# Linear attention and a routed attention layer on one core: casts in SBUF moved to ScalarE and GpSimd, constants moved, fewer warming products, other first loads, a new order

## The chip, the core and the metric

The kernel runs on one core of a Trainium2 chip. The metric is the device time of one execution in microseconds (us); the median of three runs of the kernel before is 534.78 us (534.38 to 536.3). Engines are called PE (TensorE; PEld is its weight load), VectorE (DVE in the rows), ScalarE (ACT), GpSimd (POOL) and SyncE (SP, whose queue issues most DMAs).

## The reference

Two layers follow each other. `qt`, `kt` below are q and k, laid out by the host with the head dimension first; all data is float32.

```python
def phi(x):                                    # 8 batches, 8 heads, 576 rows, head dim 64
    proj = einsum('bhsd,df->bhsf', x, w_phi)   # 128 features
    proj = proj - max(abs(proj), axis=-1, keepdims=True)
    return concatenate([exp(proj), exp(-proj)], axis=-1)
q_p, k_p = phi(q), phi(k)
kv  = einsum('bhsf,bhsd->bhfd', k_p, v);  z = sum(k_p, axis=2)
x   = (q_p @ kv) / (q_p @ z + 1e-6)            # heads side by side: 8 x 576 x 512
logits = x @ w_gate                            # 4 experts, the best 2 of a row, softmax over the 2
for e in range(4):
    q, k, v = x @ wq[e], x @ wk[e], x @ wv[e]
    a  = causal softmax(q @ k.T / 8)
    ye = a @ v @ wo[e]
    out += weight of e for this row (0 if not chosen) * ye
```

## The kernel before

The first layer is done for 32 pairs of heads p (4 pairs to a batch). For k: products with w_phi (`stream_k` for 1024 rows, `stream_tail` for the last 128), on VectorE the maxima of |proj| (L410) and their subtraction (L412), on ScalarE two exponentials (L189), then the products with v (`stream_kv`, L424 and L488). For q: a product with w_phi (`stream_q`; for p below 5 straight from float32, from p = 5 on with q split in a high and a low part, cast at L502 and subtraction at L183), copies from PSUM (`evac_u`), a maximum over partitions on GpSimd (L532), its subtraction (L542), two exponentials, and the products with kv (`stream_n`). `divide` normalises (L455, L464), `turn_x` transposes on VectorE (L577), writes to HBM and reads back as x, casts x to its high part (L589) and subtracts for the low part (L591, in L183). The second layer is done for 8 batches b: projections of q, k, v and the gate from x in high and low parts (L178), scores (L675), softmax (`soft`, `post`, with maxima on GpSimd at L532, subtractions at L806), products with v, `norm_y`, `move_y` (transpose, HBM, cast to the high part at L863, subtraction at L865), `project_out` and `store`. Weights are loaded in pieces and split likewise (`split_piece`).

What a cast in SBUF may run on is asked of `copies_sb` (L205); before it is the same as `copies`, ScalarE or VectorE. The cast of q (L500) asks `copies`, and so do copies from PSUM.

The order of the work is written out. Each piece of work is a generator ("stream") that yields its steps. `Plan.loop` reads the string PICKS two letters at a time: the first letter says which of the streams that are alive goes on (by its place in the list), the second which PSUM banks a step gets or, where a step leaves the engine open, whether it takes the first (a value below 8) or the second. At the start the streams stand in this order: A load_phi, B keep_warm, C load_k, D load_q, E load_v, F stream_k, G stream_tail, H stream_q, I to K the weights, then kv, n, s; a stream that ends leaves the list. `in_order` then holds each engine, and the queue SP, to this order. A reduction on GpSimd also waits for the last VectorE operation marked `port` ahead of it (L530).

Before the loop VectorE sets up constants: memsets (L212 to L273), and 14 operations that make `ident` and `mask` (L215 to L227; the tile is written into ek1). `keep_warm` issues groups of three products of a constant tile (L341); with WARM_AT the first four pairs' k products stand behind such groups.

How often each open choice falls on an engine by the two lists:

| operation | before | after |
|---|---|---|
| cast of x | ScalarE 27, VectorE 5 | ScalarE 12, GpSimd 20 |
| cast of y | ScalarE 12, VectorE 2 | ScalarE 5, GpSimd 9 |
| cast of q (pairs 5 to 31) | ScalarE 20, VectorE 7 | ScalarE 20, VectorE 7 |
| pieces of qk and wo | ScalarE 5, VectorE 1 | ScalarE 4, GpSimd 2 |
| pieces of vg | ScalarE 2 | ScalarE 2 |
| 64-column scaling of x | ScalarE 45, VectorE 19 | ScalarE 41, VectorE 23 |

The first real products on PE by the lists. Before: ten warming groups, q0, k0, the tail of k0, eight warming groups, q1, q2, k1, tail 1, kv0, tail 2, k2, num0, kv1. After: eight warming groups, k0, tail 0, q0, q1, q2, k1, tail 1, kv0, tail 2, k2, num0, kv1. Ahead of the first projection (after kv7 and the tail of k8) both lists hold the same products.

## Time and profile before

| | |
|---|---|
| median of three runs | 534.78 us (534.38 to 536.3) |
| the profiled execution: span from its first to its last instruction | 532.6 us; the page gives no time beside the span |
| busy | PE 522.5, PEld 505.7, DVE 496.5, ACT 389.6, POOL 195.5 us |
| granted TensorE clock | 1.000 |

In the rows below, times are us from the span's start unless marked ns. A line of a timeline merges like instructions (x is their count) and may end with the idle time of the engine before it and what released it. A group line gives busy time and the mean ns of one. PE's ends are modelled, so a busy PE is not PE at its peak.

### The profile page before, as it was taken

How to read it: one execution, taken by the hardware profiler on the slowest of the kernel's cores; microseconds unless marked ns; L12 is line 12 of the kernel's file. 1: busy time of each engine (PE TensorE's matmuls, PEld its weight loads, DVE VectorE, ACT ScalarE, POOL GpSimd, SP SyncE). 2: the span in 40 equal slices, each digit the busy share in tenths (PEclk: the TensorE clock that was granted, in tenths of full speed). 3: DMA queues.
4: the chain of work that ended last, by engine and by line, in shares of the span. 5: the costliest groups of instructions: out<-in, count | busy, mean ns of one | idle time of the engine just before them, and what ended most of it. 6: DMA issues, size and time to landing. Idle time of an engine off the chain costs nothing. (4 is left out here: it accounts for less than half of the span.)

```text
span 532.6 us, 22043 instructions
## 1 busy us (share of the span) xinstructions
PE 522.5 (98%) x9452; PEld 505.7 (95%) x9452; DVE 496.5 (93%) x1061; ACT 389.6 (73%) x723; POOL 195.5 (37%) x76
## 2 busy tenths in 40 slices
...
GB/s 203 200 202 181 199 151 118 97 146 123 147 162 100 147 77 164 188 148 191 105 114 163 106 119 169 116 199 132 117 99 159 121 82 127 112 122 101 69 90 90
DMA packets 102674, 72.68 MB, mean 136 GB/s; under 512 B 57137, under 2 KB 84145, under 8 KB 102577
## 3 DMA queue, kind: packets, MB, share of 16 engines
...
q8 instruction: 74, 1.21, 1.0%
q10 hardware_dynamic: 384, 0.39, 0.3%
...
## 5 line engine op out<-in xcount | busy, mean ns | idle before, releaser
L532 POOL PARTITION_ALL_REDUCE mx<-u x32 | 126.9, 3985 | 139.6 <-ACT u L187 54.1
L178 PE MATMUL ps_c<-xb,qk 128*128 128x320 f32 (+1 forms) x768 | 109.0, 296 | 0.0
L178 PEld LDWEIGHTS ps_c<-xb,qk 128*128 128x128 f32 x768 | 103.0, 188 | 1.5 <-issue 0.2
L189 ACT ACTIVATE ek<-ek 128x1152 f32<-128x1152 f32 x64 | 74.8, 1170 | 5.6 <-DVE ek L412 3.8
L424 PE MATMUL ps_c<-v_in,ek 128*64 128x65 f32 x2048 | 72.0, 222 | 1.7 <-ACT ek L189 1.4
L424 PEld LDWEIGHTS ps_c<-v_in,ek 128*64 128x64 f32 x2048 | 67.5, 137 | 3.5 <-ACT ek L189 1.8
L532 POOL PARTITION_ALL_REDUCE tops<-top x15 | 54.2, 3612 | 45.0 <-DVE top L714 22.0
L189 ACT ACTIVATE st<-st 128x1152 f32<-128x1152 f32 (+3 forms) x60 | 50.8, 872 | 15.4 <-DVE st L806 15.4
L806 DVE TENSOR_TENSOR st<-st,tops 128x1152 f32<-128x1152 f32 (+4 forms) x75 | 58.3, 812 | 3.0 <-POOL tops L532 2.9
L187 ACT COPY st<-ps_c 128x512 f32<-128x512 f32 (+1 forms) x101 | 45.9, 510 | 15.7 <-DVE ps_c L701 9.8
L187 ACT COPY u<-ps_c 128x320 f32<-128x320 f32 (+3 forms) x120 | 44.3, 416 | 13.7 <-PE ps_c L515 9.2
L178 PE MATMUL ps_c<-yh,wo 128*128 128x256 f32 (+1 forms) x256 | 53.0, 299 | 0.3 <-ACT yh L187 0.3
L178 PE MATMUL ps_c<-vg,xb 128*128 128x260 f32 x384 | 50.2, 284 | 0.0
L424 PE MATMUL ps_c<-vl,st 128*64 128x65 f32 x1500 | 48.8, 222 | 0.0
L412 DVE TENSOR_TENSOR ek<-ps_c,pmax 128x128 f32<-128x128 f32 (+1 forms) x64 | 47.5, 745 | 1.4 <-PE ps_c L424 0.6
L410 DVE TENSOR_REDUCE pmax<-ps_c 128x8 f32<-128x1024 f32 (+1 forms) x64 | 47.5, 747 | 0.9 <-PE ps_c L370 0.2
L178 PEld LDWEIGHTS ps_c<-vg,xb 128*128 128x128 f32 x384 | 47.9, 188 | 0.4
L424 PEld LDWEIGHTS ps_c<-vl,st 128*64 128x64 f32 x1500 | 47.1, 138 | 0.5 <-issue 0.2
L542 DVE TENSOR_TENSOR u<-u,mx 128x1152 f32<-128x1152 f32 x32 | 43.5, 1360 | 0.1
L178 PEld LDWEIGHTS ps_c<-yh,wo 128*128 128x128 f32 x256 | 40.8, 188 | 1.2 <-ACT yh L187 0.4
L189 ACT ACTIVATE u<-u 128x1152 f32<-128x1152 f32 (+3 forms) x36 | 40.7, 1139 | 0.6 <-DVE u L806 0.4
L424 PE MATMUL ps_c<-kv,u 128*64 128x65 f32 x1152 | 39.8, 222 | 0.8 <-issue 0.8
...
## 6 DMA issues: line engine op xcount, KB each, us to landing
...
q_in<-in_qt_dram SPq DMA_DIRECT2D x58, 144.0 KB, 3.3
...
k_in<-in_kt_dram SPq DMA_DIRECT2D x31, 160.0 KB, 3.6
...
```

The costliest lines, as they stand in the source:

```text
L178: nc.tensor.matmul(o, a, b, start=start, stop=stop, skip_group_check=True)
L187: nc.scalar.copy(o, i)
L189: nc.scalar.activation(o, i, func, **kw)
L410: nc.vector.tensor_reduce(out=m, in_=src, axis=AX.X, op=ALU.max, apply_absolute_value=True)
L412: nc.vector.tensor_tensor(out=to, in0=src, in1=m.unsqueeze(len(m.shape)).to_broadcast([*m.shape, 128]), op=ALU.subtract)
L424: nc.tensor.matmul(o, a, b, start=start, stop=stop, skip_group_check=True)
L532: nc.gpsimd.partition_all_reduce(o, i, 128, op)
L542: dve(2 * S, [uk], [mk], port=True).tensor_tensor(out=U, in0=U, in1=M, op=ALU.subtract)
L806: dve(2 * n, [sj[j]], [*key, mk], port=True).tensor_tensor(out=a, in0=a, in1=tops[x][0:m, :, 128 * j:], op=ALU.subtract)
```

## The change

- `copies_sb`, the choice for casts of x, y and weight pieces in SBUF, becomes ScalarE or GpSimd (`copies_sb`, `copy`); the loop takes the engine from the step's own pair.
- Memsets of tri, cnt, v_in, xq, yq and vl move from VectorE to GpSimd. The 14 operations for `ident` and `mask` stay on VectorE, but are issued by the first step of `stream_b(0)`, into a tile of the scores.
- WARMS is 8 instead of 18, and no k product waits for a warming group.
- k of pair 0: upper half and tail part on SP, lower half on ScalarE's queue (all three on ScalarE's before). q of pair 0: its second head on ScalarE's queue.
- PICKS is another list.

```diff
@@ -31,8 +31,8 @@
 XT_RATE = 1.085
 IB = 2
 Q0 = 5
-WARMS = 18
-WARM_AT = (7, 11, 14, 17)
+WARMS = 8
+WARM_AT = ()
 
 
 NPAIRS = B * NP
@@ -51,49 +51,49 @@
 
 CODE = "ABCDEFGHIJKLMNOPQRSTUVWXYZabcdefghijklmnopqrstuvwxyz0123456789-_!#$%&()*+,./:;<=>?@[]^`{|}~' §¶µ¿¡ßæøåçðþ"
 PICKS = (
-    "BADAAABABABABABABAIAIIBABAIACABAHIAAJAOAHaQIPAF-GAAANIIACACAIAHAABOAHAABABABABABABABOAOANAAAFIOICAFaNADAMAFsFIGANAQADANI"
-    "D-AACAMAMAPAGAOABAQAQAOAMAMANAECJDJAEAAAJIGAOAPAOADADADsPAOAOADADAK-CAKAJAJAEBOAOAOAOAOIFaFsBAMAJAGAPAAABASASICAD-QAQAMA"
-    "FsHATAFaAAMAGASAOANAPAPAQADAOAMAMADADIFIFAJFJAPABAK-KAJACAECNAPAOAOAJDJAQACATAQASAQAMAPAJAPIFsFIPASAFARADAAAPADADaRAK1KA"
...
+    "BEBHBEBABFBFBBBGAABACACACAHAEsBAFDOAAAAANACAFIF-NANAFaFININANAF-RAPAGAAAMAOIMAFaNIDARAHACADAGAPIMADIEFPABAAABANAOAJEJAEH"
+    "MAQAPAQAOAPAGAJAMADAHADADaOAPAOAOADADAKsKAOAOAOIMAJGJAECCAFIFjJAD-GATARAOAHAAAQASIGARAOABAQAFjFIMASAUACAAAGARAPAOAQAOAJF"
+    "JANAQAMAPAFADADAFADaEBK-KAQAJARAQAJAJAFsFaBAPAMAMAQACAAAMACAHAPAPAPAJANAPAGAUAPANADASADAOADIEDK-KAUAFIQIFAQAQANAJCJAQASA"
...
 )
 
 
@@ -138,7 +138,7 @@
             s, x = self.streams[CODE.index(i)], CODE.index(x)
             assert s[1].pred is None or s[1].pred()
             if isinstance(s[1].eng, tuple):
-                s[1].eng = 'DVE' if x >= 8 else 'ACT'
+                s[1].eng = s[1].eng[x >= 8]
             if not self.advance(s, self.take(s[1], x) if s[1].tag else None):
                 self.streams.remove(s)
         assert not self.streams
@@ -196,50 +196,52 @@
     def copy(eng, n, o, i, w, r, rate=1.04):
         if eng == 'ACT':
             act(n, o, i, w, r)
+        elif eng == 'POOL':
+            nc.gpsimd.tensor_copy(o, i)
         else:
             dve(n, w, r, rate, rate < 1).tensor_copy(o, i)
 
     def copies(n):
         return 'ACT', 'DVE'
 
-    copies_sb = copies
+    def copies_sb(n):
+        return 'ACT', 'POOL'
 
     def load(o, i, w, r=(), rate=90.0):
         nc.sync.dma_start(o, i)
 
     ek2 = [sb(f"ek{i}", [128, 2, NU, 128]) for i in range(EKB)]
-    col, row, warm = ek2[1][:, 0, 0], ek2[1][:, 0, 1, 0:32], ek2[1][:, 1, 8, 0:64].bitcast(BF16)
+    warm = ek2[1][:, 1, 8, 0:64].bitcast(BF16)
     nc.vector.memset(warm, 1.0)
     for i in range(BANKS):
         nc.vector.memset(plan.both[:, i, NJ * V1 - 1:512], 0.0)
-    nc.vector.memset(col[:, 0:1], 0.0)
-    for k in range(7):
-        n = 2 ** k
-        nc.vector.tensor_scalar(out=col[:, n:2 * n], in0=col[:, 0:n], scalar1=float(n), scalar2=None, op0=ALU.add)
-    nc.vector.transpose(row, col[:, 0:32])
-    for k in range(1, 4):
-        r_ = slice(32 * k, 32 * k + 32)
-        nc.vector.tensor_scalar(out=row[r_, 0:1], in0=row[r_, 0:1], scalar1=32.0 * k, scalar2=None, op0=ALU.add)
-    ident = sb("ident", [128, 128])
-    nc.vector.tensor_scalar(out=ident, in0=col, scalar1=row[:, 0:1], scalar2=None, op0=ALU.is_equal)
-
-    mask = sb("mask", [128, 128])
-    nc.vector.tensor_scalar(out=mask, in0=col, scalar1=row[:, 0:1], scalar2=-1.0e9, op0=ALU.is_lt, op1=ALU.mult)
-    tri = sb("tri", [128, 4, 4])
-    nc.vector.memset(tri, 0.0)
+    ident, mask = sb("ident", [128, 128]), sb("mask", [128, 128])
+    tri, cnt = sb("tri", [128, 4, 4]), sb("cnt", [128, 5, 4])
+    nc.gpsimd.memset(tri, 0.0)
     for a in range(3):
-        nc.vector.memset(tri[:, a, a + 1:4], 1.0)
-    cnt = sb("cnt", [128, 5, 4])
+        nc.gpsimd.memset(tri[:, a, a + 1:4], 1.0)
     for e in range(4):
-        nc.vector.memset(cnt[:, :, e:e + 1], float(3 - e))
+        nc.gpsimd.memset(cnt[:, :, e:e + 1], float(3 - e))
+
+    def constants(col, row):
+        nc.vector.memset(col[:, 0:1], 0.0)
+        for k in range(7):
+            n = 2 ** k
+            nc.vector.tensor_scalar(out=col[:, n:2 * n], in0=col[:, 0:n], scalar1=float(n), scalar2=None, op0=ALU.add)
+        nc.vector.transpose(row, col[:, 0:32])
+        for k in range(1, 4):
+            r_ = slice(32 * k, 32 * k + 32)
+            nc.vector.tensor_scalar(out=row[r_, 0:1], in0=row[r_, 0:1], scalar1=32.0 * k, scalar2=None, op0=ALU.add)
+        nc.vector.tensor_scalar(out=ident, in0=col, scalar1=row[:, 0:1], scalar2=None, op0=ALU.is_equal)
+        nc.vector.tensor_scalar(out=mask, in0=col, scalar1=row[:, 0:1], scalar2=-1.0e9, op0=ALU.is_lt, op1=ALU.mult)
 
     k_in = [sb(f"k_in{i}", [128, KC]) for i in range(IB)]
     q_in = sb("q_in", [128, S])
     v_ins = [sb(f"v_in{i}", [128, 10, V1]) for i in range(2)]
     for t in v_ins:
-        nc.vector.memset(t[:, :, 64:V1], 1.0)
+        nc.gpsimd.memset(t[:, :, 64:V1], 1.0)
         for h in range(2):
-            nc.vector.memset(t[64 - 64 * h:128 - 64 * h, 8 + h, 64:V1], 0.0)
+            nc.gpsimd.memset(t[64 - 64 * h:128 - 64 * h, 8 + h, 64:V1], 0.0)
     wf = sb("wf", [128, WP])
     wfs, qs = sb("wfs", [128, 2, WP], F32R), [sb(f"qs{n}", [128, S], F32R) for n in "hl"]
     kv = [sb(f"kv{i}", [128, 4, V1]) for i in range(2)]
@@ -253,7 +255,7 @@
     xd = [dp.tile([128, S], F32, name=f"xd{i}") for i in range(2)]
     xt = [sb(f"xt{i}", [128, 4, 32 * NJ]) for i in range(2)]
     for t in xq:
-        nc.vector.memset(t[64:128, :, 128:160], 0.0)
+        nc.gpsimd.memset(t[64:128, :, 128:160], 0.0)
     xB = [sb(f"xb{i}", [128, 2, S], F32R) for i in range(PXB)]
     xT = [[t[:, n] for n in range(2)] for t in xB]
     xE = sb("xe", [128, NP, 128], F32R)
@@ -265,12 +267,12 @@
     yt = [sb(f"yt{i}", [128, 4, 32 * NJ]) for i in range(2)]
     yd = [dp.tile([128, S], F32, name=f"yd{i}") for i in range(2)]
     for t in yq:
-        nc.vector.memset(t[64:128, :, 128:160], 0.0)
+        nc.gpsimd.memset(t[64:128, :, 128:160], 0.0)
     q2 = [sb(f"q{p}", [128, S], F32R) for p in "hl"]
     kk2 = [sb(f"kk{p}", [128, S], F32R) for p in "hl"]
     vl = sb("vl", [128, NJ, 4, 66])
-    nc.vector.memset(vl[:, :, :, 65:66], 1.0)
-    nc.vector.memset(vl[64:128, NJ - 1], 0.0)
+    nc.gpsimd.memset(vl[:, :, :, 65:66], 1.0)
+    nc.gpsimd.memset(vl[64:128, NJ - 1], 0.0)
     lg = vl[:, :, :, 0]
     vlo_ge = sb("vlo", [128, 4, 65])
     vlo, ge = vlo_ge[0:64], vlo_ge.rearrange("p a b -> p (a b)")[:, 0:80].rearrange("p (t a b) -> p t a b", t=5, a=4)
@@ -349,11 +351,11 @@
 
     def load_k():
         for p in range(NPAIRS):
-            yield Step('SP' if p else 'ACT', pred=(lambda: ('main_k', p - IB) in done and ('tail_k', p - IB) in done) if p >= IB else None)
-            x, q = k_in[p % IB], nc.sync if p else nc.scalar
-            q.dma_start(x[0:64, :], kt[p][:, 0:KC])
-            q.dma_start(x[64:128, 0:512], kt[p][:, 768:1280])
-            q.dma_start(x[64:128, 512:KC], kt[p][:, 640:768])
+            yield Step('SP', pred=(lambda: ('main_k', p - IB) in done and ('tail_k', p - IB) in done) if p >= IB else None)
+            x = k_in[p % IB]
+            nc.sync.dma_start(x[0:64, :], kt[p][:, 0:KC])
+            (nc.sync if p else nc.scalar).dma_start(x[64:128, 0:512], kt[p][:, 768:1280])
+            nc.sync.dma_start(x[64:128, 512:KC], kt[p][:, 640:768])
             done.add(('load_k', p))
 
     def raw_q(p):
@@ -363,7 +365,7 @@
         for p in range(NPAIRS):
             yield Step('SP', pred=(lambda: ('proj_q', p - 3) in done) if 3 <= p < Q0 else has('proj_q', Q0 - 2) if p == Q0 else has('split_q', p - 1) if p > Q0 else None)
             for h in range(2):
-                load(raw_q(p)[64 * h:64 * h + 64, :], qt[p][:, S * h:S * h + S], ('q_in', h), rate=60.0)
+                (nc.sync if p or not h else nc.scalar).dma_start(raw_q(p)[64 * h:64 * h + 64, :], qt[p][:, S * h:S * h + S])
             done.add(('load_q', p))
 
     def half_mm(o, a, b, n, w, r):
@@ -741,6 +743,8 @@
 
         left = [13]
         yield Step('PE', (), None, all_x(b * NP))
+        if b == 0:
+            constants(st[0][1][:, 0, 0:128], st[0][1][:, 0, 128:160])
         for g in range(2):
             for sel in range(2):
                 for s0, s1 in PARTS:
```

## Rows read from the trace of the kernel before

**Rows 1.** The page, part 1: busy us, share of the span, instructions.
```profile
PE 522.5 (98%) x9452; PEld 505.7 (95%) x9452; DVE 496.5 (93%) x1061; ACT 389.6 (73%) x723; POOL 195.5 (37%) x76
```
**Rows 2.** Busy time by stage: PE, PEld, DVE, ACT, POOL, granted clock, DMA share, GB/s.
```profile
15.08:66.02 50.94, 49.02 (x1273) 45.99 (x1271) 48.50 (x87) 46.68 (x74) 27.77 (x7) 1.00 0.78 195
66.02:529.36 463.34, 461.88 (x8068) 449.76 (x8066) 434.75 (x917) 336.31 (x638) 163.65 (x64) 1.00 0.49 128
```
**Rows 3.** Waits of PE: who for whom, us in total, times, longest.
```profile
PE ps_c L424 <- ACT ek L189: 1.4, 1, 1.4
```
**Rows 4.** Timeline of 54 to 67 us: start, us, engine, line (VectorE, GpSimd, PE).
```profile
56.50 0.45 DVE L200 CAST xb<-xb 128x576 fp32r<-128x576 f32 x1
...
57.20 2.67 DVE L200 CAST xb<-xb 128x576 fp32r<-128x576 f32 x1
59.79 1.21 DVE L410 TENSOR_REDUCE pmax<-ps_c 128x8 f32<-128x1024 f32 x1
...
57.12 4.15 POOL L532 PARTITION_ALL_REDUCE mx<-u  x1 [4.38 <-ACT u L187]
...
63.51 1.15 PE L424 MATMUL ps_c<-v_in,ek 128*64 128x65 f32 x32 [1.40 <-ACT ek L189]
```
**Rows 5.** Timeline of the first 16 us.
```profile
1.13 0.53 ACTq L354 DMA_DIRECT2D k_in<-in_kt_dram  x1
1.29 3.36 PE L178 MATMUL ps_c<-ek 128*128 128x128 bf16 x30 [1.29 <-DVE ps_c L214]
...
2.75 1.42 DVE L218 TENSOR_SCALAR ek<-ek 128x1 f32<-128x1 f32 x7
...
5.03 0.28 DVE L227 TENSOR_SCALAR mask<-ek 128x128 f32<-128x128 f32 x1
...
6.49 0.27 PE L370 MATMUL ps_c<-wf,k_in 64*128 64x128 f32 x1
...
7.23 0.46 DVE L200 CAST qk<-ot 128x576 fp32r<-128x576 f32 x1
...
9.47 1.50 PE L178 MATMUL ps_c<-ek 128*128 128x128 bf16 x24 [1.05 <-DVE u L200]
...
10.08 1.42 DVE L410 TENSOR_REDUCE pmax<-ps_c 128x8 f32<-128x1024 f32 x2
...
13.92 1.07 PE L370 MATMUL ps_c<-wf,k_in 64*128 64x128 f32 x16
...
15.08 1.07 PEld L424 LDWEIGHTS ps_c<-v_in,ek 128*64 128x64 f32 x32
```
**Rows 6.** DMA issues: count, KB each, median us from issue to landing.
```profile
q_in<-in_qt_dram SPq DMA_DIRECT2D x58, 144.0 KB, 3.3
...
k_in<-in_kt_dram ACTq DMA_DIRECT2D x1, 160.0 KB, 4.4
```
**Rows 7.** Groups by form: busy us, mean ns, idle before.
```profile
L577 DVE STREAM_TRANSPOSE xt<-xq 128x640 f32<-128x640 f32 x32 | 26.5, 832 | 0.6 <-ACT xq L189 0.6
L455 DVE TENSOR_TENSOR xq<-ps_c,rd 128x256 f32<-128x256 f32 x64 | 25.8, 416 | 0.5
...
L187 ACT CAST xb<-xb 128x576 fp32r<-128x576 f32 x27 | 18.0, 673 | 0.6 <-DMA xb<-xd 0.4
...
L464 DVE TENSOR_SCALAR xq<-ps_c,rd 64x64 f32<-64x64 f32 x19 | 5.2, 276 | 0.2
```
**Rows 8.** GpSimd's copies (ns min/median/max), and one beside a VectorE subtraction.
```profile
L689 POOL COPY top<-st x15: 396/462/764, 84.6 to 494.0; 128x256 f32<-128x256 f32 x15
...
L792 POOL COPY gw<-gw x8: 179/317/1177, 100.5 to 517.3; 64x2 f32<-64x2 f32 x8
...
160.65 1.35 DVE L542 TENSOR_TENSOR u<-u,mx 128x1152 f32<-128x1152 f32 x1
...
160.86 1.18 POOL L792 COPY gw<-gw 64x2 f32<-64x2 f32 x1 [0.79 <-DVE gw L789]
```
**Rows 9.** Timeline of the end, PE.
```profile
521.71 0.50 PE L178 MATMUL ps_c<-yh,wo 128*128 128x256 f32 x2 [0.30 <-ACT yh L187]
```

More of the change, by code (lines that the diff above doesn't have):

```diff
@@ new lines @@
+    "rArAqApAFIrAY-mApApAnAsADAqAqApApADArALAKAKACAmAmADalAPAOBLAlAlAQEPFnAoAKAoAjAlAlAmAfAgAfAjAeAFAmAKAiAFAMBOHfAkAlAcALAMG"
+    "LCiAdAdAdAcAdAdAdAIsEDIAdAjAjAdAjAfAiAHGHADAHAHDfAAAfAgAeIgAZABAaAAAgAgALAgAfAEHIsIAZAhAKAiAiAiAhAaIGILADAbAcAdAaAeAeAeA"
+    "JAHAEG7ALALAbAbAbAbAHA6A5A5ALs7A5ALa9A9AD-5A5A5I6A6AFaFI9A8AbAbALsLa7A7A6A6AFADAaIDADI7AaAeGdH4AAACACA9A5A9A6A9A5A5A5A9A"
+    "FA6AdBcABAKA3A3A6A2A2A5ADA4AFsFa9AYA5ADAFA3AzA0AyAZA2AD-6A4IzA2A0A2AHBHAHAzAzAIaHEEFzAHAIA3AzA2AzAHAIIIAI-5AAAFA3AzA3A3A"
@@ new lines @@
+    "3I3A3I2AzAzAzAzAzaEE4AZAYAXABAwAIA0AyAWAWACADAyA2A1A1A1ADA1AzAzAzA1A1IzAwAwAwAwA0A0AFsF-2A2I2A2A0A0A0AhIhsh-wA3A6A5A5Ahs"
+    "zADazA3AFAGAFA7A1A3A1A3A6A1A0AdAaB3A0AzA0AWAzAzAzAcAXCsAbD0IYHpAzA0ADAuAvAzAyAoAAAoIoAxAYAxIpAqACAAAYGsAvAvAuAuAnAGAGAqA"
+    "YAWAJArAXFlADADR,AqA+ABAmAFjF-.AoAnAHAHACAnA.A.A.AmAHA.AlImIXAoAFApApApApApAHDHAI-IAHApApA*AXApApA)AXAosEAoA)AIaoAmAoA(A"
+    "FA+AEBoAIA(A*AkA(A.ADA(ADAHAHAmA(A*A+A*A,A,A,A*A*A*I*A(AXRX-+A)I,ADsGA)IGA*A*AFIFa+I+A.A,A+AkA.AW-WIpDAACABA*AFA+A+A+A,A"
@@ new lines @@
+    "FABA(A)AmC&A)A(A)A,A(A)A,A)AmFDA+A&A_A)AFjFI,A+A,A&AlA_A(A(AKHkGLEFA7A#IFAFaFI-A&A$A%A%ADA&A_A_A_A_A$A_A_A_A_A_ADsHaHAEB"
+    "GH*A$A)A9AAABAGAGA-AFA$A!A&A%A7A9ACAhA9A7A9I9A9A9A9A!A$AFA$A!A$A8AgABACAAAHsEH#A#ADA_A_I_A%A6A_AHA$A$ADA$A9A#A#I#A#AmAFa"
+    "$A-AD-qsFR!A8AnA%A7A%A&AlBJCKA9A3A9A8I8Am-DA!A8A8A_AFIFAFa-A9A8A6A7A-A9A9ADAmsmI9A8IF-8A8I8I!A2A!A9A!A1IDaGGGAEH9A9A8A8A"
+    "JAdABAxAQAwA5A9A5AwA8A3A8AKFIAeEMAKBLDcCGIJA`AuA1AAAyADA[A@IaDtACApArA>AvAwA>A>AwA?AvAYHvAvAvAvAvA=AFIyAZAvAXG<ADAXDDIHs"
@@ new lines @@
+    "HAFA=AXAoA=A=A=A:A<A<A<A/AqAqIXA:AnA:AsApAoAoAAAGCGAGAssGGGAqA/AGAmIKABAsAWApAlAmAmI*A)AkAoACAmAHaEG(A(ADAEAHAmAmAmA(A)A"
+    "mAH-HA*A(A(A&A+A&A&AlA(AkA%ADAGCGAFI&A&I)AGAJAAA#A(A(I%A%A&A&IF-VsDa)A*A(A(AFI)A#ACAFA)A)AVIF-+A+A*A,A+AVsFIV-)A+ABADA)A"
+    ")A)A*A)I#A)A+AFA+ADA)ADanBkAAAMEkF%I%A%AKGJH%A&A&A%A&A&A%AgAeA5ACAeA7A8AeB7A8AECGD6AFA#A!A!AGAEEH-HA6A8A8A8A8A8A8A8A%A!A"
+    "8A-A2AGA_A#A_A2A9I8A8A8A8A8A!A9A8A4A9A8ADADA8A8A8IFa_I_Aoso-oa#A#A_A_A_A9A9A9A9A9I_AD-7AFs!AoI!A!AKE%AjFeE0AzAJAAAJA8A5A"
@@ new lines @@
+    "6A7A5A5A7A0AKGfH0A2A2A3A3AMDJCtIwADA8A6AYAxAwAwAyAyAzAZHKB4A2IYCBAvAuA0IwAwAwAyAwAZDYG1AFAxAuAuA0I1AXCtAoAH1HA1AtAtAsAuA"
+    "vAxAJACAmApAWAWAIAFAWAoAmAGAGApIWAmAtAJAlABArAqAnAqAojGApIkApAEH*AoAlIoIoAmADAnAlACAmAmAHIHAkImAmA&A%A%A%AmA%I%A(A(AGCGA"
+    "%AGAjA&A&A&A&AVIV-FaVskA*A*AF-+A(A(I(I)A)A)A*IFAVI)A(A&A(A&ADaFA)A)AKG,A(A%A%A*A&A&AnHmGmEMFJAjBAA!A7A#A!A-A9A!AiACA7AAA"
+    "7A-ADADA#A&A9A$ADa!A!A#AGHEGGAHs-AGA-A-A-A#A-A9A!A!AHAHa!A--HA!A9A9A9A_A_ADADA-A-I-AEBBAiAhA8A8A8AAA8A!A-A-A-A-I-A7A#A!A"
```

60 lines of the change are left out of this document (20 added, 40 removed).

## The prediction

> **What bounds the kernel now.** I read the page's table of busy shares first, then the busy time by stage, then who waited for whom, then the timelines of the stretch before the first projection and of the first 16 us. The table shows PE at 98% of the span and its weight loads at 95%, VectorE at 93%, ScalarE at 73%, GpSimd at 37% [rows 1]. PE is the bound over all, and a change that leaves its products as they are wins only where PE has holes. By stage [rows 2], PE is busy for 461.88 of 463.34 us from the first projection (66.02) to its last product (529.36): no hole worth a name, though VectorE is close behind with 434.75. The holes lie before 66 us. From 15.08 to 66.02 PE, VectorE and ScalarE are all above 91%, so that a stall of any of the three reaches PE.
>
> **What holds the stage before 66 us.** The largest single wait of PE with real work is 1.4 us for an exponential of k [rows 3]; it is the idle time in front of the products of kv at 63.51 [rows 4]. Followed back on VectorE: its cast of x at 57.20 took 2.67 us where the one at 56.50 took 0.45; GpSimd's reduction had started at 57.12; the maxima of k for pair 7, at 59.79, were queued behind that cast, then their subtraction, the exponential and PE behind these [rows 4]. So one cast in SBUF by VectorE cost VectorE 2.67 - 0.45 = 2.2 us and PE 1.4. At the start, VectorE's real work begins at 7.23 with the cast of a weight piece and reaches the first maxima of k only at 10.08; the first weight load of kv is at 15.08 [rows 5].
>
> The Trainium skill, "SBUF — State Buffer", section "Who interferes with whom", says that VectorE's copies and casts in a two-port mode, and its operations with two SBUF inputs, exclude a GpSimd operation that reads SBUF, and that the second to start waits until the first is done. The trace agrees that there is such a wait, not that it lasts to the end: the cast was done at 59.87, the reduction at 61.27.
>
> **The change, part by part.** Which operation runs where, and in what order, I read from the two lists of picks against the streams.
>
> 1. *First loads.* The list puts pair 0's k first: its main and tail products, then q0, q1, q2. Before, wf and the three parts of k were issued one behind the other on ScalarE's queue, k from 1.13 on, and the k products started at 6.49 [rows 5]. Now the upper half of k is first on SP, with the tail part behind it, and the lower half stands second on ScalarE's queue, where the first part of k was issued at 1.13. Landing took 4.4 us for such a part and 3.3 for one of q [rows 6], so k is there at 4.4 to 5.6. Its 20 products take about 1.4 us (the 16 of pair 1 took 1.07, [rows 5]) or twice that at half the clock: VectorE's first work comes at 6.0 to 8.0, against 7.23; taken -0.3. What is pushed back on SP are the weight pieces; v and pair 1's k come sooner than before, since fewer weight pieces stand ahead of them.
>
> 2. *VectorE's work before the first projection.* Both lists do the same products on PE before it, so VectorE's lists can be set side by side. Out go five casts: a weight piece 0.46, q5 and q8 2 x 0.46, x0 0.45 and x1 2.67, together 4.50 [rows 4, 5]. In come a cast of q6, 0.46, and the 14 operations for ident and mask, which ran from 2.66 to 5.31, thus 2.65 [rows 5]. That is -1.39. Copies from PSUM balance (one of u in, one of kv out). Four scalings of 64 columns fewer at 0.28: -1.1 [rows 7]. Put off until after the projection: a division's two multiplications at 0.42 and four smaller operations, about 1.8; drawn ahead: one transpose, 0.83; net -0.9 [rows 7]. Sum: **-3.4**. The memsets given to GpSimd are worth nothing of themselves, since VectorE had no data until about 7 us. The constants are the bad half: they leave a time in which VectorE had nothing else and enter one where it is full; the list has them behind the subtraction for pair 7's k, so that neither they nor a cast of x stand ahead of the exponential that PE waited for.
>
> 3. *Casts on GpSimd.* By the list 20 of 32 of x, 9 of 14 of y and 2 of weight pieces; ScalarE loses 15 of x and 7 of y, 22 x 0.67 = 15 us [rows 7]. A cast of 128x576 on GpSimd is not in the trace. From the nearest rows, 64x2 in 0.18 us and 128x256 in 0.40, it comes to 0.67 on a line through both, and in proportion to the second's median of 0.46 to 1.04 [rows 8]. I take 0.75, near the line, whose ends are the undisturbed runs. That GpSimd waits for VectorE is seen: the copy of 64x2 took 1.18 us beside a two-input subtraction of 1.35 [rows 8]. That such a subtraction waits for a copy is not in the trace: 0 to 1.04 us for each. Four of the casts lie before the first projection (x0, a weight piece, x1, x2): 0 to 4.2, taken **+0.7**, as subtractions are about a third of VectorE's operations there. The other 27 lie in the body, where x is cast for the next batch, and VectorE is idle for 463.34 - 434.75 = 28.6 us: taken 0. Behind a cast on GpSimd mostly a reduction is queued; GpSimd is idle for 63%.
>
> By the skill's rule every cast that a subtraction meets would hold it for the rest of the cast; with all four met in full, 4 x 0.75 = 3.0 instead of 0.7, the forecast would be 534.2.
>
> 4. *Warming products.* 24 instead of 54. The granted clock of the rows is 1.00 throughout [rows 2], but the first 30 took 3.36 us, 112 ns each, which is 128 columns at about 1.2 GHz, and the 24 at 9.47 took 1.50 us, 62 ns, the level of 2.4 GHz [rows 5]. Now they end at about 1.29 + 24 x 0.112 = 4.0, 0.4 to 1.6 us before k. The rise may come later, which costs 0 to 1.4 us, held in item 1's range. The second bundle filled a hole, and leaving it out gains nothing.
>
> 5. *PE's side.* The chain to the first products of kv, from k's products done at 6.9 in VectorE's new order: small maxima, a small subtraction, small centring, a copy, and at 8.4 the maxima (1.2), a copy (0.48) and the centring (1.2), done at 11.4; the exponential (1.17) at 12.6; kv at 12.9 against 15.08: -2.2. With the 1.4 us of [rows 3] gone too PE could be 3.6 ahead at the projection; VectorE's sum allows 0.3 + 3.4 - 0.7 = 3.0. The smaller holds, less some idle time of VectorE between 7 and 9 us, where it follows PE closely: **-2.7**.
>
> 6. *The end.* Two output products of the batch before now stand in front of the transposes of the last y; PE waits 0.3 us for a cast there [rows 9]: **-0.2**. What follows PE's last product, a copy and the store, stays.
>
> Sum: -2.9 on a span of 532.64, so 529.7. The page gives no time beyond the span; the median of the runs, 534.78, stands 2.14 above it, and with the same 2.14 the forecast is **531.9 us**.
>
> **Rivals.**
> - *The gain is eaten.* Waits for GpSimd's casts and the constants take back VectorE's saving (item 3 at +2.5): for it, VectorE is at 95% there [rows 2]; against it, the list puts the constants where x is still on its way. -1.1: 533.7. Chance 0.21.
> - *The body gets denser too.* ScalarE has 15 us less to do, and no cast of x on VectorE meets a reduction. Against it: PE shows only 1.5 us of idle time there. Another -3: 528.9. Chance 0.13.
> - *The clock stays low.* If PE pauses too much until about 12 us, its some 5 us of products ahead of kv run at half rate, most of it hidden behind VectorE: +2, 533.9. Chance 0.07.
> - *Slower: the last x of a batch.* Its cast stands on GpSimd behind a reduction of 3.9 us [rows 4], or blocked by VectorE, and VectorE's subtraction and the next projections wait for it. At 0.9 us of PE in each of 7 batches: +6.3 - 2.9, 538.2. From 0.4 us a batch on the sign turns. For it: PE and VectorE are both full. Against it: six buffers of x give half a batch of lead. Chance 0.13.
> - *Not what the words say.* The diff leaves the line of q's cast (L500) between ScalarE and VectorE, and the list gives VectorE 7 of 27, as before: no time of its own, but a meeting like that at 57.20 stays possible for q.
>
> **Numbers.** The forecast has 0.46. About 0.5%, 2.7 us, is what a measurement of this kernel can tell from no change. Of the forecast's own spread (529.5 to 533.5) two thirds lie below 532.1, which with the denser body gives faster 0.44; the slower rival and the tails of the others give slower 0.17; the rest is 0.39. Range 528.0 to 537.0: low with items 2 and 5 in full and a part of the denser body, high with five batches of the slower rival.
>
> **What would show it.** k's first product at about 5 us and kv at about 13; no VectorE cast of x, and no hole of PE ahead of pair 7's kv; the first projection at 63 to 64; GpSimd's casts at 0.7 to 0.8 us with VectorE's subtractions of x still at 0.75; from there to PE's last product 463 us, as before. It is wrong if that last stretch differs by more than 2 us either way, or the first projection stays at 66.

## The result and the profile after

The changed kernel took **540.62 us** (median of 4 runs, 540.09 to 541.59); the kernel before took 534.58 us beside it. The ratio is 1.0108, with an interval from 1.0081 to 1.0135: 6 us slower, where 531.9 was forecast. The time lies outside the range given.

The page of the kernel after, its span and its table of busy time, answers to [rows 1]: VectorE has 3 us more than before, and ScalarE 16 us less.

```profile
span 539.7 us, 22005 instructions
PE 526.3 (98%) x9422; PEld 506.7 (94%) x9422; DVE 499.7 (93%) x1038; ACT 373.9 (69%) x695; POOL 220.5 (41%) x127
```

The first projection came as early as forecast. From the timeline of the kernel after: k's first products at 5.04, the first small maxima of k at 7.69, the products of kv at 13.67 (their first weight load at 13.56, against 15.08), the first projection at 63.15 against 66.02 [rows 2, 4, 5]. No cast of x runs on VectorE. The constants (L230) stand on VectorE just ahead of the projections.

```profile
5.04 2.08 PE L372 MATMUL ps_c<-wf,k_in 64*128 64x128 f32 x16
7.69 0.29 DVE L412 TENSOR_REDUCE pmax<-ps_c 128x1 f32<-128x128 f32 x1 [5.03 <-PE ps_c L426]
...
13.67 1.10 PE L426 MATMUL ps_c<-v_in,ek 128*64 128x65 f32 x32
...
58.26 2.49 DVE L230 TENSOR_SCALAR st<-st 128x1 f32<-128x1 f32 x7
58.74 1.34 POOL L200 CAST xb<-xb 128x576 fp32r<-128x576 f32 x2
...
63.15 3.02 PE L178 MATMUL ps_c<-xb,qk 128*128 128x320 f32 x15
```

The body is where the time went. Before, it took 463.34 us from the first projection to PE's last product [rows 2]; after, that last product ends at 536.35, so it took 536.35 - 63.15 = 473.2 us. The busy times by stretch show where. Two rows of the kernel after, 143 to 190 us and 190 to 529, and behind them the first of these stretches of the kernel before; columns are PE, PEld, DVE, ACT, POOL with their instructions, the granted clock, the DMA share and GB/s:

```profile
143.00:190.00 47.00, 43.21 (x785) 41.37 (x786) 44.78 (x84) 32.52 (x62) 18.12 (x8) 0.96 0.38 103
190.00:529.36 339.36, 337.41 (x5858) 327.72 (x5854) 318.82 (x680) 222.92 (x422) 131.58 (x67) 1.00 0.47 126
```
```profile
143.00:190.00 47.00, 46.44 (x931) 45.15 (x931) 45.02 (x90) 39.98 (x75) 18.29 (x7) 1.00 0.51 129
```

In these 47 us PE did 785 products instead of 931 (not all of the same kinds; the table further down weighs them), with 3.8 us of holes and part of the stretch at a lower clock. The timeline of the kernel after there, from top to bottom: a reduction of GpSimd starts at 145.27, and y's subtraction, 0.41 us behind it, takes 2.30 us. A second reduction starts at 155.44, and the third subtraction of the scores, on 64x128, takes 2.52 us; the same line is done in 0.27 elsewhere. The centring of k (161.73) is queued on VectorE behind it, PE waits for that 2.16 us, and then its products run at half rate (56 in 3.08 us, against 1.84 in the first run below); the granted clock of the 7 us from 164 is 0.76.

```profile
145.27 3.58 POOL L534 PARTITION_ALL_REDUCE tops<-top  x1 [2.67 <-DVE top L716]
...
145.68 2.30 DVE L869 TENSOR_TENSOR yl<-yl,yh 128x576 fp32r<-128x576 f32 x1
...
150.56 1.16 PE L372 MATMUL ps_c<-wf,k_in 64*128 64x128 f32 x16 [0.93 <-DVE kkl L183]
...
155.44 4.64 POOL L534 PARTITION_ALL_REDUCE mx<-u  x1 [6.59 <-ACT kv L187]
...
156.20 2.52 DVE L810 TENSOR_TENSOR st<-st,tops 64x128 f32<-64x128 f32 x1
...
161.73 1.21 DVE L414 TENSOR_TENSOR ek<-ps_c,pmax 128x1024 f32<-128x1024 f32 x1
...
163.08 1.27 PE L426 MATMUL ps_c<-kv,mx 128*64 128x65 f32 x36 [2.16 <-DVE ek L414]
...
164.15 3.08 PE L426 MATMUL ps_c<-vl,st 128*64 128x65 f32 x56
```
```profile
164.00:171.00 7.00, 7.00 (x186) 7.00 (x183) 5.38 (x19) 2.96 (x5) 0.00 (x0) 0.76 0.35 88
```

GpSimd's casts took what was expected for x, and more for y; from its groups by line (times, mean ns, idle before and its releaser):

```profile
L200 POOL CAST xb<-xb 128x576 fp32r<-128x576 f32 x20 | 15.2, 767 | 62.7 <-DMA xb<-xd 34.6 <-issue 11.3 <-PE ps_c L517 9.0
L200 POOL CAST yh<-yl 128x576 fp32r<-128x576 f32 x9 | 9.4, 1048 | 11.0 <-DMA yl<-yd 11.0
```

### The profile page after: what moved, and what is told of

Same layout as the page of the kernel before. It is cut to its first block, busy times and chain, and to the rows that moved or that the text cites. A ratio compares the mean times of both kernels' runs of the same rounds, so it can differ in the third digit from the quotient of the medians.

```text
span 539.7 us, 22005 instructions
## 1 busy us (share of the span) xinstructions
PE 526.3 (98%) x9422; PEld 506.7 (94%) x9422; DVE 499.7 (93%) x1038; ACT 373.9 (69%) x695; POOL 220.5 (41%) x127
## 4 chain that ended last, share of the span: by engine, by line
PE 80%; DVE 11%; ACT 3%; issue 2%; DMA 1%; SPq 1%; POOL 1%; DVEq 0%; ACTq 0%
PE ps_c L178 34%; PE ps_c L426 28%; PE ps_c L677 7%; PE ps_c L372 5%; PE ps_c L517 4%; DVE st L810 2%; PE ps_c L490 2%; DMA xb<-xd 1%; ACT ek L189 1%; DVE xt L579 1%; SPq L211 1%; DVE pmax L412 1%; PE ps_c L513 1%; POOL tops L534 1%; DVE ek L414 1%
## 5 line engine op out<-in xcount | busy, mean ns | idle before, releaser
L810 DVE TENSOR_TENSOR st<-st,tops 128x1152 f32<-128x1152 f32 (+4 forms) x75 | 61.6, 861 | 0.9 <-POOL tops L534 0.7
L187 ACT COPY st<-ps_c 128x288 f32<-128x288 f32 (+1 forms) x102 | 45.4, 499 | 22.4 <-DVE ps_c L703 16.3
L412 DVE TENSOR_REDUCE pmax<-ps_c 128x1 f32<-128x128 f32 (+1 forms) x64 | 47.5, 746 | 6.0 <-PE ps_c L426 5.7
L178 PE MATMUL ps_c<-yh,wo 128*128 128x320 f32 (+1 forms) x256 | 52.7, 298 | 0.1
L426 PE MATMUL ps_c<-vl,st 128*64 128x65 f32 x1500 | 50.9, 226 | 1.0 <-issue 0.5
L187 ACT COPY u<-ps_c 128x320 f32<-128x320 f32 (+3 forms) x116 | 42.0, 412 | 13.5 <-PE ps_c L517 6.2
L426 PEld LDWEIGHTS ps_c<-vl,st 128*64 128x64 f32 x1500 | 48.6, 141 | 2.2 <-issue 0.7
L544 DVE TENSOR_TENSOR u<-u,mx 128x1152 f32<-128x1152 f32 x32 | 45.3, 1416 | 0.3 <-POOL mx L534 0.3
L426 PE MATMUL ps_c<-kv,mx 128*64 128x65 f32 x1152 | 39.6, 223 | 2.2 <-DVE ek L414 2.2
L200 POOL CAST xb<-xb 128x576 fp32r<-128x576 f32 x20 | 15.2, 767 | 62.7 <-DMA xb<-xd 34.6
```

The lines of the kernel that those rows point to most:

```text
L178: nc.tensor.matmul(o, a, b, start=start, stop=stop, skip_group_check=True)
L187: nc.scalar.copy(o, i)
L412: nc.vector.tensor_reduce(out=m, in_=src, axis=AX.X, op=ALU.max, apply_absolute_value=True)
L426: nc.tensor.matmul(o, a, b, start=start, stop=stop, skip_group_check=True)
L544: dve(2 * S, [uk], [mk], port=True).tensor_tensor(out=U, in0=U, in1=M, op=ALU.subtract)
L810: dve(2 * n, [sj[j]], [*key, mk], port=True).tensor_tensor(out=a, in0=a, in1=tops[x][0:m, :, 128 * j:], op=ALU.subtract)
```

## The experiments

Theory L, formed from these rows: the new order puts VectorE's operations with two inputs in SBUF right behind the start of GpSimd's reductions, which hold them; the casts on GpSimd are harmless. Rival C: GpSimd's casts cost the time. Rival O: the new order costs it by itself, whatever VectorE does. Later rivals came with what the runs showed.

All orders below are lists of picks; each kernel is its whole list encoded anew.

For comparing orders, this table was worked out from the traces. Each step of PE counts the time that a quick step of its kind takes in the kernel before (its 20th percentile), in the order in which the kernel does it. The table gives how much later (+) than the kernel before each kernel has done the same sum of work, in us, each from one execution. That one can be slower than the median of its run, so that the last column is not the timed difference: "later" was traced at 540.58 us where its median is 537.98, "behind" at 544.43 (540.69), "old 130-245" at 548.22 (544.77). The names: "later", "behind" and "lined up" are the three repairs further down; "old order, 8" is the code after with the order before and 8 groups of warming products, the two lines below it add the casts and then the 18 groups; "old start" and the three lines below it are joined from the two orders.

```
before at     15.3   66.0   81.7  128.0  143.6  190.8  253.7  529.3
after         -1.5   -2.9   -1.7   -1.5   -1.1   +4.5   +4.3   +7.0
y marked      -1.2   -1.3   -0.3   -0.2   +0.3   +2.8   +3.2   +3.4
later         -1.7   -1.6   +0.1   +0.2   +0.7   +3.3   +3.4   +5.9
behind        -1.4   +1.3   +3.0   +3.1   +3.6   +8.0   +8.0   +9.9
lined up      -1.1   -2.5   -0.9   -0.8   -0.3   +1.9   +1.8   +4.8
on ScalarE    -2.3   -0.7   -0.5   +2.1   +2.6  +11.1  +11.6  +15.1
casts alone   -0.1   +1.1   +2.5   +2.5   +2.4   +2.4   +2.2   +2.4
old order, 8  +2.3   +1.6   +3.7   +3.7   +3.6   +3.3   +3.2   +3.5
 and casts    +1.9   +0.6   +1.3   +1.3   +1.2   +1.7   +1.8   +2.9
 and 18       +0.3   +0.4   +0.4   +0.4   +0.3   +1.0   +0.7   +1.2
old start     +0.2   -0.5   +1.1   +1.3   +1.8   +6.1   +6.8   +9.0
new to 130    -1.5   -2.6   -1.0   -0.8   +1.0   +0.3   +0.6   +0.8
old 130-245   -1.5   -0.8   +0.9   +1.0   +3.3   +2.5   +9.2  +13.4
new 130-245    0.0    0.0   +3.6   +3.6   +3.8   +9.2  +12.6  +12.0
```

**y marked.** The reductions wait for the last VectorE instruction that is marked; y's subtraction was not.

```diff
         yield Step('DVE', [('yh', g, 0)], hot=True)
+        plan.port = len(nc.cur_bb.bb.instructions)
         nc.vector.tensor_tensor(out=lo, in0=to, in1=hi.bitcast(F32), op=ALU.subtract)
```

> The changed kernel, with y's subtraction (L869) counted among the operations that a later reduction on GpSimd waits for. Theory L (a subtraction with two SBUF inputs that VectorE reaches within the first two us of a reduction is held until those are over): the subtraction that took 2.30 us at 145.68 takes 0.75 again, PE's hole at 150.56 (0.93 us) goes, and 540.6 falls to 536.5 to 539, lower if the second hold (156.20, 2.52 us) goes with the shift. Rival C (the casts on GpSimd themselves cost the time): no change, 540 to 541.5. Rival O (the new order of PE's work costs it): no change.

538.69 us, ratio 1.0068 (1.0041 to 1.0094). Its timeline: the subtraction takes 0.74, the reduction waits for it and starts at 147.85. The second hold stays in full: the four subtractions of the scores from 153.91 on take 5.52 us, against 3.28 in the first repair below, and PE waits 1.97 us behind them. But its clock stays full afterwards, and the 56 products take 1.84.

```profile
147.01 0.74 DVE L870 TENSOR_TENSOR yl<-yl,yh 128x576 fp32r<-128x576 f32 x1
...
147.85 3.58 POOL L534 PARTITION_ALL_REDUCE tops<-top  x1 [3.92 <-DVE yl L870]
...
153.91 5.52 DVE L810 TENSOR_TENSOR st<-st,tops 128x1152 f32<-128x1152 f32 x4
...
162.88 1.27 PE L426 MATMUL ps_c<-kv,mx 128*64 128x65 f32 x36 [1.97 <-DVE ek L414]
...
163.95 1.84 PE L426 MATMUL ps_c<-vl,st 128*64 128x65 f32 x56
```
```profile
143.00:190.00 47.00, 44.68 (x847) 42.93 (x847) 45.86 (x90) 35.57 (x67) 19.30 (x10) 1.00 0.41 111
```

The median is 1.9 us lower. The two intervals overlap a little (1.0081 to 1.0094), so the size is not sharp. By the table the loss from 128.0 to 190.8 falls from 6.0 to 3.0 us; a part of that is the clock, which is at half in the one execution and full in the other. Against "old start", which has the hold and a full clock there (4.8), it falls by 1.8.

**Casts on ScalarE.** The changed kernel, its 31 casts on GpSimd given to ScalarE.

```diff
     def copies_sb(n):
-        return 'ACT', 'POOL'
+        return 'ACT', 'ACT'
```

> The changed kernel and its order, with the 31 casts that it gives to GpSimd on ScalarE, none on GpSimd. Theory L: the reductions start as they did, so the holds at 145 and 156 stay, within 2 us of 540.6 (538 to 542). Rival C: the loss goes, 533 to 535. Rival O: 540 to 541.

550.71 us, ratio 1.0299 (1.0263 to 1.0335): the holds stay with no cast on GpSimd, as Theory L expected, but the time grows by 10 us, where -2.6 to +1.4 was expected. ScalarE stands 4.66 us at a cast whose x is still on its way (164.28), the exponentials of gates and scores are behind it, and PE waits 5.34 us for them.

```profile
149.34 2.30 DVE L869 TENSOR_TENSOR yl<-yl,yh 128x576 fp32r<-128x576 f32 x1
...
168.38 0.70 PE L426 MATMUL ps_c<-vl,st 128*64 128x65 f32 x8 [5.34 <-ACT st L189]
```

So the holds are not the work of GpSimd's casts. What these casts cost by themselves the run does not tell, since it gives ScalarE a wait that it did not have. The trace of the kernel after bounds it: VectorE's operations beside GpSimd's casts are longer than usual by 3.2 us in the whole body, 0.55 of it from 128.0 to 190.8, where PE loses 6.0.

**New start, old body; old start, new body.** The lists were joined at the first projection, with some PSUM banks given anew.

```diff
-PICKS: changed kernel's list
+first run:  changed kernel's steps 0 to 304, then the rest in the order of the kernel before
+second run: steps 0 to 320 of the kernel before, then the rest in the changed kernel's order
```

> The changed kernel up to the first projection (its loads, constants, 8 warming groups and order), then the order and the engines of the kernel before (x and y cast on VectorE where that one did). Theory L, by which the start gains 1.9 us and the body loses 8.9: 532 to 533.5. If the new start carries the loss to later stages (the constants in VectorE's way, other loads): 535 or more.

540.84 us, ratio 1.010 (1.0069 to 1.013): missed. VectorE is held in its body only once, for 0.45 us near the end (518.4), and still it is slow. The loss is nearly all at the join: counted as in the table it stands at -3.3 at 66.0, at +6.2 at 81.7 and at +8.2 at the end. From 66 to 84 us PE is busy 13.98 of 18 us, and its clock is 0.88:

```profile
66.00:84.00 18.00, 13.98 (x121) 13.04 (x123) 11.89 (x27) 7.65 (x19) 7.88 (x2) 0.88 0.54 126
```

The two orders had done different things by step 305, and the join left PE waiting. It says little of the body.

> The reverse: the kernel before up to its first projection (its loads, constants, 18 warming groups), then the order and the engines of the changed kernel, its casts on GpSimd too. Theory L with the body's own loss of about 8.9 us: 540.5 to 544. If the loss came from the start or only from how the two fit at that instant: 533 to 537.

543.6 us, ratio 1.016 (1.0136 to 1.0185), as expected; the holds came again in full, 1.56, 2.25 and 1.15 us over the usual times.

**The parts without the order.** The changed kernel's code with the order, banks and engines of the kernel before. First: new first loads, late constants, GpSimd's memsets, 8 groups.

```diff
-        return 'ACT', 'POOL'
+        return 'ACT', 'POOL', 'DVE'
 # PICKS: the list of the kernel before, without warming groups 8 to 17
```

> The code of the changed kernel (first loads, constants made later, GpSimd's memsets, 8 groups of warming products) with the order, the PSUM banks and the engines of the kernel before, casts on VectorE included. Theory L (the loss is VectorE's subtractions that the new order puts into the first 2 us of GpSimd's reductions; the parts themselves cost nothing): 532.5 to 535.5 us, within 0.4% of the kernel before, no long subtraction beside a reduction's start but the one cast at 57 us. Rival S (8 groups and the new loads leave TensorE idle or at half clock at the start, and that costs): 536 to 539 us, with TensorE's first projection later than 67 us.

538.66 us, ratio 1.0076 (1.0049 to 1.0104). Rival S was nearer. Products that take 1.2 to 1.3 us at full clock take 2.17 as late as 7.61 us, and q's 16 at 11.98 take 4.21. The cast at 58.75 is held as before, and the late constants come behind it: the first projection is at 67.56, and by the table PE is 3.7 us late at 81.7.

```profile
7.61 2.17 PE L372 MATMUL ps_c<-wf,k_in 64*128 64x128 f32 x16 [0.65 <-DMA k_in<-in_kt_dram]
...
11.98 4.21 PE L513 MATMUL ps_c<-st,wf 64*128 64x320 f32 x16 [1.58 <-DVE ek L414]
15.98 1.27 PE L372 MATMUL ps_c<-wf,k_in 64*128 64x128 f32 x16
...
58.75 2.67 DVE L202 CAST xb<-xb 128x576 fp32r<-128x576 f32 x1
...
65.47 1.43 DVE L230 TENSOR_SCALAR st<-st 128x1 f32<-128x1 f32 x7
```

Then the same with VectorE's 8 casts on GpSimd, the whole change but its order:

> As the run above, and the 8 casts in SBUF that the order gave to VectorE are GpSimd's: the whole change but its order and its other choices of engine. Theory L: 531.5 to 535 us, since the cast held 2.2 us at 57 us is gone from VectorE and GpSimd's casts stretch VectorE's work by 0.2 to 0.5 us each at most. Rival C (casts on GpSimd cost more than they free): slower than the run above by 1.5 us or more.

537.88 us, ratio 1.0057 (1.0036 to 1.0079). The hold is gone and PE is 2.4 us earlier at 81.7 than in the run above, as the table shows; against the kernel before it is still slower. Then that run with the 18 groups of before:

```diff
-WARMS = 8
+WARMS = 18
```

> As the run of the whole change but its order (537.88 us, 8 groups of warming products, full clock granted from 15.8 us of the span), with the 18 groups of the kernel before at their old places. Theory W (with the old order the 10 groups left out let the clock stay at half, 1.9 us by 17 us): full clock from 5 to 7 us, 535.5 to 536.5 us. Rival (the first loads and the late constants carry the loss, the groups nothing): 537.5 to 538.5 us.

535.93 us, ratio **1.0002** (0.9977 to 1.0027). The same products now take 1.25 and 2.23 us:

```profile
7.78 1.25 PE L372 MATMUL ps_c<-wf,k_in 64*128 64x128 f32 x16 [1.35 <-DMA k_in<-in_kt_dram]
...
12.06 2.23 PE L513 MATMUL ps_c<-st,wf 64*128 64x320 f32 x16 [1.06 <-DVE ek L414]
```

So with the old order the 10 groups left out cost 0.5%, and everything else in the change but its order, taken together, costs nothing that can be measured. In the new order k's second pair, at 12.31, already takes 1.16; no run has the new order with 18 groups.

**Casts alone.** The kernel before with nothing but those 8 casts on GpSimd.

> The kernel before with its 8 casts in SBUF that VectorE had given to GpSimd, and nothing else. From the pair of runs with the old order (the cast held at 57 us cost TensorE's first projections some 2.4 us, and all 8 casts together 0.8 us net in the medians): 532 to 534.3 us, 0.5 to 2.5 us faster than the kernel before, TensorE ahead by 1 to 2 us from 70 us on. Rival C (casts on GpSimd give back what they free): 534.5 to 536 us.

535.64 us, ratio 0.9987 (0.9959 to 1.0016): no change that can be measured, and a time in rival C's range; that the casts themselves took the time back, the trace does not show. The maxima of k are at 57.60 instead of 59.79 [rows 4], 0.08 us behind the reduction's start and not held; their input is in PSUM. In this execution PE waited 1.83 us for v's DMA instead:

```profile
57.52 3.94 POOL L535 PARTITION_ALL_REDUCE mx<-u  x1 [3.33 <-DVE u L545]
57.60 1.22 DVE L413 TENSOR_REDUCE pmax<-ps_c 128x8 f32<-128x1024 f32 x1
...
64.63 1.16 PE L427 MATMUL ps_c<-v_in,ek 128*64 128x65 f32 x32 [1.83 <-DMA v_in<-in_v_dram]
```

**Repairs of the stretch at 150 to 170 us.** All three have y marked. The first moves one reduction of GpSimd behind the third subtraction of the scores.

```diff
-POOL reduce u14, cast x9, cast x10 | ACT ... | DVE scores 0, 1, 4, 2, gates, scores 3, centre k14
+POOL cast x9 | ACT ... | DVE scores 0, 1, 4, 2 | POOL reduce u14, cast x10 | DVE centre k14, gates, scores 3
```

> The changed kernel with y's subtraction marked, so that reductions wait for it, and with one reduction (the one that starts at 155.4 us) moved behind the third subtraction of the scores that it held, that fourth column's centering of k one place earlier. Theory L: the hold of 2.25 us, TensorE's idle 2 us at 162.8 go: 535 to 536.5 us, 2 to 3.5 us under the marked kernel (538.7), TensorE level with it up to 150 us and ahead from 165 us. Rival O (the order itself starves TensorE there, whatever VectorE's holds): 538 to 539.5 us, TensorE idle at 160 to 164 us as before.

537.98 us, ratio 1.0052 (1.0034 to 1.007): between the two. The hold moved to two operations of the gates, which take 0.17 each when free (the second ends with the reduction, at 162.1), and PE waited 1.8 us.

```profile
158.17 3.94 POOL L534 PARTITION_ALL_REDUCE mx<-u  x1 [5.74 <-DVE st L810]
...
159.46 1.18 DVE L789 SCALAR_TENSOR_TENSOR gw<-gt 128x20 f32<-128x20 f32 x1
...
160.88 1.25 DVE L791 TENSOR_SCALAR gs<-gs 128x5 f32<-128x5 f32 x1
```

The second moves the reduction behind the gates and the last subtraction too:

```diff
-DVE scores 0, 1, 4, 2 | POOL reduce u14, cast x10 | DVE centre k14, gates, scores 3
+DVE scores 0, 1, 4, 2, gates, scores 3 | POOL reduce u14, cast x10 | DVE centre k14
```

> As the run with y marked and one reduction later, with that reduction moved on behind the gates' small operations and the last subtraction of the scores, which it had held in that run (1.01 and 1.08 us), and the centering of k behind it. Theory L: no VectorE operation is held between 150 and 165 us, TensorE idle under 0.5 us there, 535 to 536.5 us. Rival O (the order starves TensorE there whatever VectorE does): 537.5 to 539 us with TensorE idle over 1.5 us between 158 and 166 us.

540.69 us, ratio 1.0079 (1.0055 to 1.0103): missed. Nothing is held in the stretch, but the subtraction that needs the reduction now stands 3.01 us at the head of VectorE's line, the last centring of k is behind it, and PE waits 2.48:

```profile
166.90 1.79 DVE L544 TENSOR_TENSOR u<-u,mx 128x1152 f32<-128x1152 f32 x1 [3.01 <-POOL mx L534]
...
170.06 1.16 ACT L189 ACTIVATE ek<-ek 128x1152 f32<-128x1152 f32 x1 [4.81 <-DVE ek L414]
171.28 0.92 PE L426 MATMUL ps_c<-v_in,ek 128*64 128x65 f32 x24 [2.48 <-ACT ek L189]
```

The third puts that subtraction behind the centring:

```diff
-DVE subtract u14, split q15, maxima k14.8, divide, centre k14.8, split x9, divide
+DVE maxima k14.8, divide, centre k14.8, divide, split q15, subtract u14, split x9
```

> As the last run of the new order (540.69 us; there the reduction behind the scores' subtractions held nothing, but VectorE stood 3.01 us at the subtraction that waits for it, with the last centering of k in line behind it, and TensorE then idle 2.48 us), with that subtraction moved behind the maximum and the centering of k's last heads, the division's first two operations and one subtraction of q. Theory L, widened (what the new order costs at 150 to 170 us is VectorE's time in line, held in a reduction's first part or standing for its end, whichever the order gives): TensorE idle under 0.7 us between 150 and 175 us, no half clock there, 535 to 537 us. Rival O (the order starves TensorE there for another reason): 538 to 540.5 us.

539.28 us, ratio 1.008 (1.0059 to 1.01): missed, though the place is mended. PE has no wait over 0.5 us and its clock is full from 140 to 180 us, and PE is busy 45.69 of the 47 us, against 43.21 in the kernel after:

```profile
143.00:190.00 47.00, 45.69 (x870) 43.52 (x870) 45.07 (x89) 35.41 (x67) 18.68 (x10) 1.00 0.40 107
```

By the table it still loses 2.7 us from 128.0 to 190.8, half of what the kernel after loses there, and 3 us behind 253.7. None of the three can be told from the mark alone (1.0068), which loses 3.0 there: with the second hold gone PE has hardly gained.

**The stretch alone.** By step 640 (130 us) the two orders have done the same but for three steps, so they can be joined there with the banks as they were.

```diff
-PICKS: changed kernel's list
+first run:  changed 0 to 639, then the order before
+second run: changed 0 to 639, before up to step 1176, then changed again
+third run:  before (18 groups) up to step 643, changed up to step 1180, then before again
```

> The changed kernel's code with its own order up to step 640 (130 us, where the two orders have done nearly the same: three steps differ) and from there the order and engines of the kernel before, banks unchanged; the casts after that point are those of the kernel before, VectorE's among them. Theory P (the new order loses nothing up to 140 us and 5 to 6 us between 143 and 186 us): 532.5 to 535 us, 0 to 0.5% faster than the kernel before. Rival Q (the loss is spread over the whole order, or already lies in the new start once its first loads vary): 536.5 to 539 us.

535.85 us, ratio **0.9998** (0.9974 to 1.0022). In the stretch PE has no hole:

```profile
143.00:190.00 47.00, 47.00 (x928) 45.78 (x928) 44.19 (x89) 40.12 (x77) 17.97 (x7) 1.00 0.50 126
```

> The changed kernel with the order and engines of the kernel before in one stretch alone, steps 640 to 1176 (130 to 245 us). Theory P: the 5 to 6 us of that stretch come back, 534.5 to 537 us, against 540.6 for the changed kernel. Rival Q: 538.5 to 541 us.

544.77 us, ratio 1.0165 (1.0126 to 1.0204): missed as a whole. The stretch itself is mended: PE busy 47.00 of 47.00, and by the table -0.8 from 143.6 to 190.8. But at the second join, at 245 us, PE waits 3.98 us for a cast of q, and the granted clock of the 8 us around it is 0.79; +6.7 lie between 190.8 and 253.7.

```profile
143.00:190.00 47.00, 47.00 (x873) 45.83 (x873) 43.93 (x87) 40.57 (x78) 16.61 (x6) 1.00 0.51 131
248.00:256.00 8.00, 4.02 (x27) 3.75 (x26) 7.00 (x12) 4.23 (x6) 8.00 (x4) 0.79 0.86 189
```
```profile
252.06 2.08 PE L372 MATMUL ps_c<-wf,k_in 64*128 64x128 f32 x16 [3.98 <-ACT qsh L187]
```

> The other way about: order and engines of the kernel before with its 18 groups of warming products, in the changed kernel's code (first loads, late constants), and the new order in steps 643 to 1180 (130 to 245 us) alone. Theory P: 5 to 6 us slower than the like kernel with the old order throughout, so 540.5 to 542.5 us. Rival Q: under 538.5 us.

545.81 us, ratio 1.0175 (1.0141 to 1.0209): more than expected. The stretch itself costs what was expected, +5.4 from 143.6 to 190.8, with the same two holds, a wait of 1.97 us and the same granted clock as in the kernel after; its second join adds 3.4. The cast held at 57 us, the constants behind it and a clock at half from 70 us had cost 3.6 ahead of it.

```profile
147.00:194.00 47.00, 43.28 (x768) 41.45 (x768) 44.87 (x84) 32.73 (x62) 19.73 (x10) 0.96 0.36 94
```
```profile
150.59 2.30 DVE L869 TENSOR_TENSOR yl<-yl,yh 128x576 fp32r<-128x576 f32 x1
161.11 2.52 DVE L810 TENSOR_TENSOR st<-st,tops 64x128 f32<-64x128 f32 x1
...
167.81 1.27 PE L426 MATMUL ps_c<-kv,mx 128*64 128x65 f32 x36 [1.97 <-DVE ek L414]
```

No run beats the kernel before: the nearest are the casts alone (0.9987) and the new order up to 130 us (0.9998), both the same as it.

## Why the prediction was wrong, point by point

**The step that failed** is the term for the body, "463 us, as before": the new order got no term of its own there and was put at nothing without a reason. The body took 473.2. Item 3 argued for the casts alone ("The other 27 lie in the body ... taken 0"), from 28.6 us of VectorE's idle time added up over the whole body; the new order was never held against GpSimd's reductions.

What the runs showed in its place: of the 9.9 us that the table gives the kernel after between 66.0 and the end, 6.0 lie from 128.0 to 190.8 and 2.7 behind 253.7. In the first of these stretches the new order loses 6.0, 4.8 and 5.6 us in the executions that have it unrepaired (after, old start, new 130-245); the old one loses 1.1 and 1.5 (new to 130, old 130-245), all of it ahead of 143.6, where the lists are joined. That it is this stretch, and that it comes with the new order there (its engines and banks included), is shown by exchanging it. Of the mechanism a part is shown: y's subtraction held by a reduction is 1.9 us of the median, 1.8 in the stretch at equal clock, and the half clock behind PE's wait is up to another 1.7 us in an execution that has it (an estimate: 24% of 7 us). The hold of the scores' subtraction costs little by itself: it stands in full in the run with y marked (3.0 us lost there), and with it repaired 2.7 are still lost. The third hold, at 279, also stands in full in the run with y marked, which loses 0.2 behind 253.7. What makes the last 2.7 us of the stretch is open, and so is the loss behind 253.7 (0.2 to 4.2 us in the executions with the new order there).

**Item 3, the casts.** The price was right for x: 0.77 us for a cast against 0.75 taken (1.05 for one of y), with VectorE's subtractions of x at 0.76 against 0.75 before. That a subtraction waits for a whole cast finds no support: in the kernel after, the largest excess of a subtraction beside a cast was 0.47 us. Additions from SBUF to SBUF did wait: the seven of the constants at 58.26 took 2.49 us beside a reduction and two casts, against 1.43 in the run of the new parts with the old order. The hold at 57.20, read as the price of a *cast*, is not the cast's own: VectorE's operations with two SBUF inputs are held alike right behind a reduction's start. Taking the cast away took one such meeting away, and the new order made three (0.41, 0.76 and 0.82 us behind the starts at 145.27, 155.44 and 278.62).

**Items 1 and 5, the start.** In the profiled execution the projection came 2.9 us earlier, against 2.7 forecast, but not by the steps worked out: VectorE's first maxima stand at 7.69, 0.5 later than its first work before, where 0.3 earlier was taken, and kv is 1.5 earlier where 2.2 was worked out. The rest is the wait of [rows 3], which is gone as forecast. By 81.7, 1.2 of the 2.9 was gone again; PE's weight loads stood 0.6 us for x's subtractions behind the constants and 0.5 for one of q. And the gain does not repeat: the seven executions that share this start stand at -1.7, -1.0, -0.9, -0.3, +0.1, +0.9 and +3.0 at 81.7. The timed run of this start with the old order behind it is equal to the kernel before. The -2.7 was the best case, taken as the likeliest, and that the traced execution met it is luck.

**Item 2.** "Neither they nor a cast of x stand ahead of the exponential" held. The constants stood ahead of x's subtraction, which the next products needed, and took 3.7 us (58.16 to 61.89) instead of 2.65; in the old order with 18 groups and the casts on GpSimd, all this sums to nothing.

**Item 4.** With the old order the 10 groups left out cost 0.5%. In the new order k's first 16 products took 2.08 us, twice the usual, as the item allowed, and its second pair 1.16; whether the groups would gain anything there is not tested.

**Item 6** was not visible: counted as in the table, the kernel after stands at +7.1 at 503 us and at +7.0 at the end.

**The rivals.** The slower one had nearly the right size (538.2) and the wrong mechanism: no projection of the body waits for a late cast of x in the kernel after. "The gain is eaten" fits what is left of the start when it is timed. "The body gets denser" was wrong in its sign, for the reason of the failed step.
